# kv of two heads in column halves of the array, and the first four q units by exponentials with sums

## The chip, the core and the metric

The kernel runs on one core of a Trainium2 chip. The engines named here are TensorE (PE in the rows; PEld are its weight loads), VectorE (DVE), ScalarE (ACT), GpSimd (POOL) and SyncE (SP, which issues the transfers). The metric is the time of one execution on the device, in microseconds (us).

## What is computed

Linear attention over 8 batches, 8 heads, 576 tokens and 64 features, followed by two MLPs (512 to 2048 to 512) over the 4608 tokens. Cut to what matters here:

```
q_s = exp(q - max(q, -1));  q_s = q_s / (sum(q_s, -1) + 1e-09)
k_s = exp(k - max(k, tokens));  k_s = k_s / (sum(k_s, tokens) + 1e-09)
kv  = einsum('bhsd,bhse->bhde', k_s, v)        # 64 x 64 for each batch and head
x   = einsum('bhsd,bhde->bhse', q_s, kv)       # then (4608, 512)
x   = leaky(x @ w_in1) @ w_out1                # leaky: max(0.01 h, h)
x   = silu(x @ w_in2) @ w_out2
```

## The kernel before

**Units.** The attention works on pairs of heads. A unit is one pair p (4 of them) in one block j of 512 tokens (9 blocks); for k and v, block j stands for batch j, so that 32 units, numbered n, have a `k_task` and a `v_task`, and 36 have a `q_task`. A `k_task` loads k of both heads of one batch as four chunks of 128 tokens plus one chunk of 64 (576 = 4 x 128 + 64), finds the maximum over tokens with two transposes on TensorE (lines 480 and 486), adds its negative (489, 494), takes the exponential (498 into `kx`, 502 for the short chunk) and multiplies with v on TensorE (508 for the four chunks, 509 for the short one) into one PSUM tile `pk`. Both heads are computed in one matmul of 128 x 129: the 64 x 64 blocks on the diagonal are the two kv, the other two blocks are not read, and column 128 is a column of ones in v, whose product is the sum of the exponentials. Lines 515 and 516 form its reciprocal, and 521 scales the two blocks into `kv`.

**q.** A `q_task` finds the maximum over the 64 features (572). For the first eight units (`n < NS`) it then adds the negative maximum (577, on GpSimd or VectorE), takes one exponential of all 512 columns (581) and sums them on VectorE (583). For later units eight exponentials of 64 columns each (592) add the negative maximum as their bias and leave the sum as well. Then come the reciprocal (598, 599), the product with it (601, GpSimd or VectorE), four transposes (608), their copy (612), the matmul with kv (623), and the split of the result into two fp32r parts `x` (631 and the helper line 292).

**MLPs.** The first layer (`layer0`) is three fp32r matmuls for each of four k-tiles (651, 652, 653), for 16 columns f of w and 9 blocks. Its weights are decoded and split on ScalarE and VectorE as they come in (329 to 346, then 296 and 292). The other three layers, from about 532 us to the end, are lines 872 and 922.

**Order.** Everything is recorded by a planner, `Queues`, that holds each engine's queue as a time line and gives the next place to the task that can start first, with costs written at each `op`. Each engine then executes its rows strictly in that order. A matmul of a side task (`"p"`) may be placed between those of layer 0.

**Buffers.** Six sets of (k, v) tiles, called `u` in the rows, are lent to the units in turn. Before the first unit GpSimd writes the ones columns of v (980) and zeros the eight `kv` tiles (982).

Of the kernel before, what the change touches and what calls it, by code (L numbers as in the profile page):

```python
# [13 lines left out]
ACTF = mybir.ActivationFunctionType  # L14
# [188 lines left out]
def linear_attention_two_mlps(  # L203
# [24 lines left out]
    nc = tc.nc  # L228
    B, H, S, D = q.shape
    NT, DM = out.shape  # L230
    DFF = w_in1.shape[1]
    P = 128
    TB = 512
    NB = NT // TB
    NP = H // 2
# [3 lines left out]
    SR = S - SM  # L239
    EPS = 1e-9  # L240
    FS = 6
    NU = 8
    NS = 8
# [18 lines left out]
    gd = [tc.dram_tile([NG, 4, P, TB], F32, name=f"gd{j}") for j in range(NB)]  # L262

    NKV = 8
    NV = 2 * D + 1
    ident = const.tile([P, P], F32, name="ident")
    ones = const.tile([P, 1], F32, name="ones")
    kvbuf = [const.tile([P, P], F32, name=f"kv{i}") for i in range(NKV)]
# [166 lines left out]
    sets = []  # L435
# [9 lines left out]
    def k_task(n):  # L445

        b, j, p = units[n]
        if n >= NU:
            yield wait(("kvs", n - NU))
        of[n] = yield get(r_kv)  # L450
        kf, vv = of[n]
        done(("set", n))
        heads = slice(2 * p, 2 * p + 2)

        yield op(("D", 0.73))
        nc.sync.dma_start(
            out=kf[:, 0:512].rearrange("p (h c) -> p h c", h=2),
            in_=k[b, heads, 0:SM, :].rearrange("h (p c) d -> p h (c d)", c=4),
        )
        kh = kf[:, 0:512].rearrange("p (h c d) -> p h c d", c=4, h=2)  # L460
        k4 = kf[:, 0:512].rearrange("p (h c d) -> p c h d", c=4, h=2)
        yield op(("D", 0.56))
        k1 = kf[0:SR, 512:640]
        nc.sync.dma_start(
            out=k1.rearrange("p (h d) -> p h d", h=2), in_=k[b, heads, SM:S, :].rearrange("h p d -> p h d")
        )
        m1 = yield get(r_m)
        m2 = yield get(r_o)
        m2v = m2[:, 0:4 * D].rearrange("p (h c d) -> p h c d", h=2, c=2)
        yield op(("V", v_tt(256)))  # L470
        nc.vector.tensor_tensor(out=m2v, in0=kh[:, :, 0:2], in1=kh[:, :, 2:4], op=ALU.max)
        yield op(("V", v_tt(128)))
        nc.vector.tensor_tensor(out=m1, in0=m2v[:, :, 0], in1=m2v[:, :, 1], op=ALU.max)
        r_o.put(m2)
        m1f = m1.rearrange("p h d -> p (h d)")
        yield op(("V", v_tt(128)))
        nc.vector.tensor_tensor(out=m1f[0:SR], in0=m1f[0:SR], in1=k1, op=ALU.max)
        pm = yield get(r_attn)
        yield op(("p", 0.12))
        nc.tensor.transpose(pm[:, 0:P], m1f, ident)  # L480
        r_m.put(m1)
        nm = small[n % NU]["k"][:, 0:1]
        yield op(("V", v_tt(128)))
        nc.vector.tensor_reduce(out=nm, in_=pm[:, 0:P], axis=AX.X, op=ALU.max, negate=True)
        yield op(("p", 0.12))
        nc.tensor.transpose(pm[:, P:2 * P], nm.to_broadcast([P, P]), ident)
        nb = pm[:, P:2 * P]
        yield op(("V", v_tt(512)))
        nc.vector.tensor_tensor(
            out=k4, in0=k4,  # L490
            in1=nb.rearrange("p (h d) -> p h d", h=2).unsqueeze(1).to_broadcast([P, 4, 2, D]), op=ALU.add,
        )
        yield op(("V", v_tt(128)))
        nc.vector.tensor_tensor(out=k1, in0=k1, in1=nb[0:SR], op=ALU.add)
        r_attn.put(pm)
        kx = yield get(r_kx)
        yield op(("A", a_(512)))
        nc.scalar.activation(
            out=kx.rearrange("p (c h d) -> p c h d", c=4, h=2), in_=k4, func=ACTF.Exp
        )  # L500
        yield op(("A", a_(128)))
        nc.scalar.activation(out=k1, in_=k1, func=ACTF.Exp)
        yield wait(("v", n), *([("xm", n - NKV + NP)] if n >= NKV - NP else []))
        vv = vv.rearrange("p (c n) -> p c n", c=5)
        pk = yield get(r_attn)
        yield op(("p", 1.1))
        for c in range(4):
            nc.tensor.matmul(pk[:, 0:NV], lhsT=kx[:, c * P:(c + 1) * P], rhs=vv[:, c, :], start=c == 0, stop=False)  # L508
        nc.tensor.matmul(pk[:, 0:NV], lhsT=k1, rhs=vv[0:SR, 4, :], start=False, stop=True)  # L509
        r_kv.put(of.pop(n))  # L510
        r_kx.put(kx)
        done(("kv", n))
        rk = small[n % NU]["k"][:, 1:2]
        yield op(("V", 0.15))
        nc.vector.tensor_scalar_add(rk, pk[:, 2 * D:NV], EPS)
        nc.vector.reciprocal(out=rk, in_=rk)
        w = kvbuf[(b * NP + p) % NKV]
        for i in range(2):
            o = slice(i * D, (i + 1) * D)
            yield op(("A", a_(64)))  # L520
            nc.scalar.activation(out=w[o, o], in_=pk[o, o], func=ACTF.Copy, scale=rk[o])
        kv[b, p] = w
        r_attn.put(pk)
        done(("kvs", n))

    def v_task(n):
        b, j, p = units[n]
        yield wait(("set", n))
        t = of[n][1]
        t = t.rearrange("p (c n) -> p c n", c=5)  # L530
        for i in range(2):
            yield op(("D", 0.73))
            nc.sync.dma_start(
                out=t[:, 0:4, i * D:(i + 1) * D],
                in_=v[b, 2 * p + i, 0:SM, :].rearrange("(p c) d -> p c d", c=4),
            )

            yield wait()
        yield op(("D", 0.56))
        nc.sync.dma_start(  # L540
            out=t[0:SR, 4, 0:2 * D].rearrange("p (h d) -> p h d", h=2),
            in_=v[b, 2 * p:2 * p + 2, SM:S, :].rearrange("h p d -> p h d"),
        )
        yield wait()
        done(("v", n))
# [9 lines left out]
    def q_task(n):  # L555

        b, j, p = units[n]
# [14 lines left out]
        nc.vector.tensor_reduce(out=nq, in_=qv, axis=AX.X, op=ALU.max, negate=True)  # L572
        sq = rq = small[n % NU]["rq"]
        x4 = qx.rearrange("p (c h d) -> p c h d", c=4, h=2)
        if n < NS:
            e = yield op(("G", 1.0), ("V", v_tt(512)))
            engines[e].tensor_tensor(
                out=qv, in0=qv, in1=nq.unsqueeze(2).to_broadcast([P, 8, D]), op=ALU.add
            )
            yield op(("A", a_(512)))  # L580
            nc.scalar.activation(out=x4, in_=q4, func=ACTF.Exp)
            yield op(("V", v_tt(512)))
            nc.vector.tensor_reduce(
                out=sq, in_=qx.rearrange("p (a d) -> p a d", a=8), axis=AX.X, op=ALU.add
            )
        else:

            for c in range(4):
                for h in range(2):
                    at, to = 4 * h + c, 2 * c + h  # L590
                    yield op(("A", 0.4))
                    nc.scalar.activation(
                        out=x4[:, c, h], in_=q4[:, c, h], func=ACTF.Exp, bias=nq[:, at:at + 1],
                        accum_out=sq[:, to:to + 1],
                    )
# [379 lines left out]
    with tc.manual_schedule():  # L975
        nc.vector.memset(ones, 1.0)
        make_identity(nc, ident)
        nc.scalar.activation(out=small[0]["k"][:, 0:1], in_=ones, func=ACTF.Exp)
        for _, t in sets:
            nc.gpsimd.memset(t.rearrange("p (c n) -> p c n", c=5)[:, :, 2 * D:], 1.0)  # L980
        for t in kvbuf:
            nc.gpsimd.memset(t, 0.0)

# [58 lines left out]
```

## Time and profile before

| | |
|---|---|
| median of 3 runs | 1631.16 us (1629.92 to 1631.63) |
| the profiled execution's own time | 1635.08 us |
| its span, first to last instruction | 1633.1 us |
| mean granted TensorE clock | 0.995 |
| TensorE busy | 1603.1 us |
| VectorE, ScalarE, GpSimd busy | 1194.2, 851.3, 39.1 us |

A row of a timeline has a start, a busy time, an engine, a line of the kernel, what it writes and reads, and a count if equal rows follow each other. A row of TensorE begins when the one before it still drains, so the distance between two starts, not the busy time, is what a matmul takes of the engine. An fp32 matmul stands as two rows in the trace, an fp32r matmul as one.

### The profile page before, as it was taken

How to read it: one execution, taken by the hardware profiler on the slowest of the kernel's cores; microseconds unless marked ns; L12 is line 12 of the kernel's file. 1: busy time of each engine (PE TensorE's matmuls, PEld its weight loads, DVE VectorE, ACT ScalarE, POOL GpSimd, SP SyncE). 2: the span in 40 equal slices, each digit the busy share in tenths (PEclk: the TensorE clock that was granted, in tenths of full speed). 3: DMA queues.
4: the chain of work that ended last, by engine and by line, in shares of the span. 5: the costliest groups of instructions: out<-in, count | busy, mean ns of one | idle time of the engine just before them, and what ended most of it. 6: DMA issues, size and time to landing. Idle time of an engine off the chain costs nothing.

```text
span 1633.1 us, 30896 instructions
## 1 busy us (share of the span) xinstructions
PE 1603.1 (98%) x11456; PEld 1501.8 (92%) x11456; DVE 1194.2 (73%) x2205; ACT 851.3 (52%) x1824; POOL 39.1 (2%) x53
## 2 busy tenths in 40 slices
PE   6899999999999999999999999999999999999999
PEld 4688888888788999999999999999999999999999
DVE  8886656657566887777788966666669877777775
ACT  5768756766445544444447433444446544444442
POOL 2101001000000000000000000000000000000000
PEclk9899999999999999999999999999999999999999
DMA  8766767777779655454558344333338544444442
GB/s 227 234 195 167 209 196 240 212 242 230 225 235 311 214 150 168 141 170 145 166 143 277 131 152 140 131 133 133 135 130 279 163 131 135 133 130 136 134 132 78
DMA packets 251030, 287.25 MB, mean 176 GB/s; under 512 B 59392, under 2 KB 182272, under 8 KB 250880
## 3 DMA queue, kind: packets, MB, share of 16 engines
q1 hardware_dynamic: 250880, 285.29, 56.6%
q8 instruction: 90, 1.47, 0.4%
q14 instruction: 60, 0.49, 0.1%
HBM read 168.82 MB, written 116.39 MB: 175 GB/s over the span
## 4 chain that ended last, share of the span: by engine, by line
PE 93%; DVE 5%; DMA 1%; issue 0%; ACT 0%; SPq 0%; DVEq 0%; ACTq 0%
PE b L922 22%; PE h L922 21%; PE b L872 11%; PE h L872 11%; PE h L651 8%; PE h L653 8%; PE h L652 8%; PE a L623 2%; PE a L508 2%; PE a L608 1%; DVE o L810 1%; PE a L509 1%; DVE a L292 1%; DVE x L292 1%; DVE g L292 0%
## 5 line engine op out<-in xcount | busy, mean ns | idle before, releaser
L651 PE MATMUL h<-x,w 128*128 128x512 f32 x576 | 238.5, 414 | 2.3 <-ACT w L296 1.6
L296 ACT ACTIVATE x<-x 128x512 fp32r<-128x512 f32 x209 | 131.8, 631 | 205.8 <-DMA x<-gda 91.0
L653 PE MATMUL h<-x,w 128*128 128x512 f32 x576 | 225.9, 392 | 1.2 <-DVE w L292 1.2
L652 PE MATMUL h<-x,w 128*128 128x512 f32 x576 | 225.4, 391 | 0.8 <-DVE x L292 0.5
L810 DVE TENSOR_TENSOR o<-o,b 128x512 f32<-128x512 f32 x190 | 128.1, 685 | 72.5 <-PE b L872 39.7
L810 DVE TENSOR_TENSOR o<-o,h 128x512 f32<-128x512 f32 x188 | 126.6, 685 | 62.7 <-PE h L872 36.7
L884 ACT ACTIVATE o<-o 128x512 f32<-128x512 f32 x144 | 89.2, 629 | 145.5 <-DVE o L810 144.7
L684 ACT ACTIVATE o<-h 128x512 f32<-128x512 f32 x144 | 85.9, 597 | 118.0 <-PE h L653 109.0
L296 ACT ACTIVATE x<-o 128x512 fp32r<-128x512 f32 x169 | 105.2, 631 | 70.0 <-DVE o L810 53.8
L922 PE MATMUL b<-a,x 128*128 128x256 f32 x1080 | 141.4, 283 | 0.1
L292 DVE TENSOR_TENSOR x<-x 128x512 fp32r<-128x512 f32 x209 | 137.2, 684 | 2.5
L651 PEld LDWEIGHTS h<-x,w 128*128 128x128 f32 x576 | 108.8, 189 | 29.2 <-ACT w L296 2.5
L922 PEld LDWEIGHTS b<-a,x 128*128 128x128 f32 x1080 | 134.7, 192 | 0.3 <-DVE x L292 0.3
L922 PE MATMUL b<-x,a 128*128 128x256 f32 x1044 | 132.0, 284 | 0.6 <-DVE x L292 0.5
L653 PEld LDWEIGHTS h<-x,w 128*128 128x128 f32 x576 | 108.4, 188 | 25.6 <-DVE w L292 2.3
L872 PE MATMUL h<-x,a 128*128 128x256 f32 x1008 | 130.0, 283 | 1.3 <-DVE x L292 1.3
L652 PEld LDWEIGHTS h<-x,w 128*128 128x128 f32 x576 | 108.9, 189 | 22.8 <-issue 1.2
L922 PEld LDWEIGHTS b<-x,a 128*128 128x128 f32 x1044 | 128.1, 192 | 1.1 <-DVE x L292 1.0
L872 PEld LDWEIGHTS h<-x,a 128*128 128x128 f32 x1008 | 124.9, 192 | 1.5 <-DVE x L292 1.5
L922 PE MATMUL h<-x,a 128*128 128x256 f32 x996 | 126.0, 283 | 0.2
L872 PE MATMUL b<-x,a 128*128 128x256 f32 x960 | 123.8, 283 | 1.3 <-DVE x L292 1.3
L922 PEld LDWEIGHTS h<-x,a 128*128 128x128 f32 x996 | 122.3, 192 | 0.7 <-DVE x L292 0.6
(116 smaller groups left out, 2819.3 us busy)
## 6 DMA issues: line engine op xcount, KB each, us to landing
gda<-o SPq DMA_DIRECT2D x144, 256.0 KB, 2.6
gd<-o SPq DMA_DIRECT2D x144, 256.0 KB, 2.6
x<-gd SPq DMA_DIRECT2D x102, 256.0 KB, 2.7
x<-gda SPq DMA_DIRECT2D x89, 256.0 KB, 2.8
a<-wc SPq DMA_DIRECT2D x84, 256.0 KB, 4.3
wc<-o SPq DMA_DIRECT2D x72, 256.0 KB, 3.2
raw<-in_moe_w_out_dram SPq DMA_DIRECT2D x32, 512.0 KB, 4.2
g<-gda SPq DMA_DIRECT2D x37, 256.0 KB, 2.7
```

What stands on the lines that cost most here:

```text
L292: engines[e].tensor_tensor(out=out_, in0=a, in1=b.bitcast(F32), op=ALU.subtract)
L296: nc.scalar.activation(out=out_, in_=in_, func=ACTF.Copy)
L508: nc.tensor.matmul(pk[:, 0:NV], lhsT=kx[:, c * P:(c + 1) * P], rhs=vv[:, c, :], start=c == 0, stop=False)
L623: nc.tensor.matmul(po, lhsT=kv[bb, p], rhs=qT.rearrange("p (c t) -> p c t", c=4)[:, :, a:e], start=True, stop=True)
L651: nc.tensor.matmul(h, lhsT=w[:, 0, kk], rhs=x[:, 0], start=kk == 0, stop=False)
L652: nc.tensor.matmul(h, lhsT=w[:, 0, kk], rhs=x[:, 1], start=False, stop=False)
L653: nc.tensor.matmul(h, lhsT=w[:, 1, kk], rhs=x[:, 0], start=False, stop=kk == KD - 1)
L684: nc.scalar.activation(out=o, in_=h, func=ACTF.Prelu, alpha=0.01)
L810: nc.vector.tensor_tensor(out=o, in0=a, in1=b, op=alu)
L872: nc.tensor.matmul(bank[:, r * HB:(r + 1) * HB], lhsT=w4[:, a, r, k], rhs=x3[:, b, k], start=n == 0, stop=n == 5,)
L884: nc.scalar.activation(out=t, in_=t, func=ACTF.Silu)
L922: nc.tensor.matmul(bank[:, m * HB:(m + 1) * HB], lhsT=s[:, a, at:at + P], rhs=x[:, b, r * HB:(r + 1) * HB], start=i + m + n == 0, stop=i = ...
```

## The change

1. In `k_task` each chunk is multiplied for each head alone: 128 tokens x 64 columns of k against 65 columns of v (64 and a one), written to partitions 0 to 63 of `pk` for the first head and 64 to 127 for the second. The built program gives these matmuls a tile of 128 rows and 64 columns of the array, at column 0 and at column 64 in turn. The v tile has the ones column behind each head, so its row is 130 wide and not 129.
2. The short chunk is computed with all 128 rows: the lower 64 rows of its k and v are filled with zeros, once, by GpSimd.
3. In `q_task` units 0 to 3 now take the way with eight exponentials; units 4 to 7 keep the old one.

```
-    NV = 2 * D + 1
+    NV = 2 * (D + 1)
...
-        for c in range(4):
-            nc.tensor.matmul(pk[:, 0:NV], lhsT=kx[:, c * P:(c + 1) * P], rhs=vv[:, c, :], start=c == 0, stop=False)
-        nc.tensor.matmul(pk[:, 0:NV], lhsT=k1, rhs=vv[0:SR, 4, :], start=False, stop=True)
+        for c in range(5):
+            kc = kx[:, c * P:(c + 1) * P] if c < 4 else kf[:, 512:640]
+            for h in range(2):
+                o = slice(h * D, (h + 1) * D)
+                nc.tensor.matmul(
+                    pk[o, 0:D + 1], lhsT=kc[:, o], rhs=vv[:, c, h * (D + 1):(h + 1) * (D + 1)],
+                    start=c == 0, stop=c == 4,
+                )
...
-        nc.vector.tensor_scalar_add(rk, pk[:, 2 * D:NV], EPS)
+        nc.vector.tensor_scalar_add(rk, pk[:, D:D + 1], EPS)
...
-            nc.scalar.activation(out=w[o, o], in_=pk[o, o], func=ACTF.Copy, scale=rk[o])
+            nc.scalar.activation(out=w[o, o], in_=pk[o, 0:D], func=ACTF.Copy, scale=rk[o])
...
-                out=t[:, 0:4, i * D:(i + 1) * D],
+                out=t[:, 0:4, i * (D + 1):i * (D + 1) + D],
...
-            out=t[0:SR, 4, 0:2 * D].rearrange("p (h d) -> p h d", h=2),
+            out=t[0:SR, 4].rearrange("p (h d) -> p h d", h=2)[:, :, 0:D],
...
-        if n < NS:
+        if NP <= n < NS:
...
-        for _, t in sets:
-            nc.gpsimd.memset(t.rearrange("p (c n) -> p c n", c=5)[:, :, 2 * D:], 1.0)
+        for t_, t in sets:
+            t5 = t.rearrange("p (c h d) -> p c h d", c=5, h=2)
+            nc.gpsimd.memset(t5[:, :, :, D:], 1.0)
+
+            nc.gpsimd.memset(t_[SR:P, 512:640], 0.0)
+            nc.gpsimd.memset(t5[SR:P, 4, :, 0:D], 0.0)
```

Because the planner places every row, the order of the first part changes on all engines. On TensorE it is the same again, but for the changed matmuls, from about row 490 of 2714 on, well before layers 1 to 3. Behind line 504 the line numbers of the changed kernel are up to 10 higher (608 becomes 614, 623 becomes 629).

On TensorE, at the beginning of the program, these rows stood in a row before (480 and 486 are the transposes of k, 508 and 509 the kv of unit 0, 608 the transposes of q):

```order
L608 MATMUL a<-ident,o_154 128x128 x4
L480 MATMUL a<-ident,m_233 128x128
L486 MATMUL a<-ident,k_130 128x128
L508 MATMUL a<-u_171,kx 128x129 x4
L509 MATMUL a<-u_171,u_170 128x129
L480 MATMUL a<-ident,m_251 128x128
L608 MATMUL a<-ident,o_157 128x128 x4
L623 MATMUL a<-uq_182,kv_111 128x512
```

and these stand there now (512 is the kv, 614 the transposes of q, 629 the product of q and kv):

```order
L480 MATMUL a<-ident,m_245 128x128
L486 MATMUL a<-ident,k_130 128x128
L614 MATMUL a<-ident,o_154 128x128 x4
L480 MATMUL a<-ident,m_265 128x128
L512 MATMUL a<-u_171,kx 64x65 x8
L512 MATMUL a<-u_171,u_170 64x65 x2
L486 MATMUL a<-ident,k_133 128x128
L629 MATMUL a<-uq_182,kv_111 128x512
```

Five matmuls of a unit's kv have become ten of half the width, and the transposes of the first q stand behind those of the second k.

On ScalarE, right at the beginning, stood before (329 and 344 belong to the decoding of w, 581 is the exponential of q, 498 and 502 those of k, 612 the copy of the transposed q):

```order
L329 ACTIVATE o_155<-rw_207 128x512
L581 ACTIVATE o_154<-uq_182 128x512
L498 ACTIVATE kx<-u_170 128x512
L502 ACTIVATE u_170<-u_170 64x128
L344 ACTIVATE rw_207<-rw_207 128x512
L612 ACTIVATE uq_182<-a 128x512
```

and stands now (598 is the exponential of 64 columns with its sum):

```order
L598 ACTIVATE o_154,rq_129<-uq_182,q_128 128x64 x4
L498 ACTIVATE kx<-u_170 128x512
L502 ACTIVATE u_170<-u_170 64x128
L598 ACTIVATE o_154,rq_129<-uq_182,q_128 128x64 x4
L329 ACTIVATE o_155<-rw_219 128x512
L598 ACTIVATE o_157,rq_132<-uq_182,q_131 128x64 x5
L618 ACTIVATE uq_182<-a 128x512
```

The eight exponentials of a unit stand around those of k, and the decoding of w comes behind them.

On VectorE, at the same place, stood before (572 is the maximum of q, 484 that of k, 489 and 494 add it to k, 583 is the sum of q, 598 and 599 its reciprocal, 471 and 473 begin the next k):

```order
L572 TENSOR_REDUCE q_128<-uq_182 128x8
L484 TENSOR_REDUCE k_127<-a 128x1
L331 TENSOR_SCALAR o_155<-o_155 128x512
L489 TENSOR_TENSOR u_170<-u_170,a 128x4x2x64
L494 TENSOR_TENSOR u_170<-u_170,a 64x128
L583 TENSOR_REDUCE rq_129<-o_154 128x8
L598 TENSOR_SCALAR rq_129<-rq_129 128x8
L599 RECIPROCAL rq_129<-rq_129 128x8
```

and stands now:

```order
L578 TENSOR_REDUCE q_128<-uq_182 128x8
L484 TENSOR_REDUCE k_127<-a 128x1
L489 TENSOR_TENSOR u_170<-u_170,a 128x4x2x64
L494 TENSOR_TENSOR u_170<-u_170,a 64x128
L471 TENSOR_TENSOR o_156<-u_172 128x256
L473 TENSOR_TENSOR m_245<-o_156 128x128
L477 TENSOR_TENSOR m_245<-m_245,u_172 64x128
L578 TENSOR_REDUCE q_131<-uq_182 128x8
L604 TENSOR_SCALAR rq_129<-rq_129 128x8
L605 RECIPROCAL rq_129<-rq_129 128x8
```

The sum of q (583) is gone for this unit, the decoding of w (331) has moved back, and the second unit's k and q have moved forward.

## Rows read from the trace of the kernel before

**Rows 1.** The page: busy time of the engines, and the chain's shares.

```profile
PE 1603.1 (98%) x11456; PEld 1501.8 (92%) x11456; DVE 1194.2 (73%) x2205; ACT 851.3 (52%) x1824; POOL 39.1 (2%) x53
PE 93%; DVE 5%; DMA 1%; issue 0%; ACT 0%; SPq 0%; DVEq 0%; ACTq 0%
```

**Rows 2.** Windows: length, busy PE, PEld, DVE, ACT, POOL (rows), clock, DMA, GB/s.

```profile
0.00:72.00 72.00, 51.29 (x207) 35.92 (x208) 60.05 (x146) 44.19 (x92) 19.84 (x36) 0.91 0.82 237
72.00:112.00 40.00, 40.00 (x180) 32.77 (x179) 34.39 (x76) 25.94 (x68) 1.08 (x1) 1.00 0.71 202
```

**Rows 3.** Groups of instructions behind 72 us: count, busy us, mean ns, idle before.

```profile
L508 PE MATMUL a<-u,kx 128*128 128x129 f32 x192 | 25.4, 275 | 0.0
L509 PE MATMUL a<-u,u 64*128 64x129 f32 x48 | 11.7, 323 | 0.0
```

**Rows 4.** Timeline of PE around the kv of one unit: start, busy us.

```profile
305.35 1.05 PE L508 MATMUL a<-u,kx 128*128 128x129 f32 x8
306.34 0.49 PE L509 MATMUL a<-u,u 64*128 64x129 f32 x2
306.75 0.50 PE L651 MATMUL h<-x,w 128*128 128x512 f32 x1
307.09 0.39 PE L652 MATMUL h<-x,w 128*128 128x512 f32 x1
307.32 0.40 PE L653 MATMUL h<-x,w 128*128 128x512 f32 x1
```

**Rows 5.** Timeline of the weight loads at the same place.

```profile
306.33 0.29 PEld L509 LDWEIGHTS a<-u,u 64*128 64x128 f32 x2
306.75 0.19 PEld L651 LDWEIGHTS h<-x,w 128*128 128x128 f32 x1
306.86 0.19 PEld L652 LDWEIGHTS h<-x,w 128*128 128x128 f32 x1
```

**Rows 6.** Timeline of PE: a short product of q and kv; a transpose and its successor.

```profile
396.28 0.33 PE L623 MATMUL a<-uq,kv 128*128 128x64 f32 x2
...
124.71 0.27 PE L480 MATMUL a<-ident,m 128*128 128x128 f32 x1
124.73 0.48 PE L651 MATMUL h<-x,w 128*128 128x512 f32 x1
```

**Rows 7.** The chain that ended last, its first 80 us: start, us.

```profile
8.60 0.61 DVE rq L583
...
21.87 1.72 PE a L508 x8
23.59 0.64 PE a L509 x2
...
32.73 0.60 DVE rq L583
...
52.30 1.83 PE a L508 x8
54.13 0.73 PE a L509 x2
...
57.71 1.28 PE a L508 x8
```

**Rows 8.** Timeline of ScalarE: two exponentials with sums in a row.

```profile
104.32 0.34 ACT L592 ACTIVATE o<-uq,q 128x64 f32<-128x64 f32 x1
104.65 0.34 ACT L592 ACTIVATE o<-uq,q 128x64 f32<-128x64 f32 x1
```

**Rows 9.** Groups of instructions before 72 us: sum of q, exponential of q.

```profile
L583 DVE TENSOR_REDUCE rq<-o 128x8 f32<-128x512 f32 x8 | 5.4, 671 | 0.2 <-ACT o L581 0.2
L581 ACT ACTIVATE o<-uq 128x512 f32<-128x512 f32 x8 | 5.0, 622 | 1.3 <-POOL uq L577 1.2
```

**Rows 10.** Timeline of GpSimd: its fills of kv, and its first product with q.

```profile
1.44 1.19 POOL L982 MEMSET kv<- 128x128 f32 x8
...
9.79 1.04 POOL L601 TENSOR_TENSOR o<-o,rq 128x512 f32<-128x512 f32 x1 [2.84 <-DVE rq L599]
```

## The prediction

> **What bounds the kernel now.** I read the page first: TensorE is busy for 98% of the span, and the chain that ended last lies on it for 93% [rows 1]. A busy TensorE is not one at its peak, so the second view is the windows. From 72 us on TensorE has no gap: 40.00 of 40.00 us with VectorE at 34.39 and ScalarE at 25.94 [rows 2]. Before 72 us it is another kernel: TensorE 51.29 of 72, VectorE 60.05, ScalarE 44.19. Third, the timeline: behind 72 us the starts on TensorE follow each other without a hole, layer 0 in steps of 0.23 us (307.09 to 307.32 in [rows 4]). So there are two accounts. Behind 72 us whatever TensorE is spared is gained one for one, as long as nothing else becomes late; before, the gain goes by the chain, which runs mostly over VectorE.
>
> How many kv products lie behind 72 us: 192 rows of the four long chunks, eight to a unit, so 24 of the 32 units [rows 3].
>
> **What the kv of a unit costs now.** In [rows 4] its first row starts at 305.35 and the first layer-0 matmul that is in step again at 307.09: 1.74 us, of which 0.23 belong to the matmul at 306.75. The kv takes 1.51 us. The eight rows of the long chunks stand for 1.05 us, the last one's own 0.275 [rows 3] included, so seven steps take 0.78 and one 0.11. Ten at this pace would be 1.11; the other 0.40 is what the 64-row chunk adds: 0.99 us from 305.35 to 306.34 where eight steps are 0.89, 0.41 for two steps of 0.11, and a late step behind it (306.75 to 307.09, 0.34 for 0.23). The array is set from 128 to 64 rows and back, and the first weights behind each change can't load under the matmul before it. That weights do load under matmuls inside the other shape is in [rows 5]: two loads of 0.19 us stand for 0.29, so the second began 0.10 behind the first, and its matmul followed as in the wide shape.
>
> **What it costs afterwards.** The 64-row shape is gone (zeros filled in), but the shape of 128 rows by 64 columns takes its place, so the two changes per unit stay; I carry over their 0.40. Of it about 0.05 goes, half of one exposed load of 0.11 us (the two loads behind the change back are 0.11 apart, 306.75 and 306.86 [rows 5]), since the first load after the change has 64 columns. Remaining 0.35. The ten rows become twenty of 65 columns. The time of a row goes with its columns: 129 take 0.11, so 65 take 0.056; the shortest fp32 product here, two rows of 64 columns, stands for 0.33 us less its last row's drain of about 0.27, again 0.06 [rows 6].
>
> No row shows two halves of the array at work, so this price is bounded. From above, if the halves take turns: 20 x 0.056 = 1.12, with 0.35 it is 1.47, 0.04 less than now. From below, if a row of the second half runs wholly under one of the first: the order in a chunk is first half, first half, second, second, so that each pair of neighbours of different halves overlaps and ten full steps are left, plus ten small ones. The smallest distance of two starts is 0.02 us (124.71 to 124.73, [rows 6]): 10 x 0.076 + 0.35 = 1.11, 0.40 less. I take the halves as working at once, because they write other partitions and hold other weights and nothing else in the rows ties them, with a small step of 0.03 rather than 0.02, since the row behind 124.73 is itself late: 10 x 0.086 + 0.35 = 1.21, which is 0.30 less per unit, times 24 = **-7.2 us**.
>
> Beside these rows, TensorE: Matmul & The Clock Gate (the Trainium skill, "Part 3: Packing small matmuls") says that matmuls in other column groups start about 4 ns behind each other; by that the ten small steps would be 0.04 us together and the unit 0.95, a gain of 13 us. TensorEngine Tiling (the Trainium skill, "Key Properties") says that changing the tiling mode, though not the tile, drains the engine; here the trace agrees, with the 0.40 above, and by it my two changes per unit stay and no further one comes between the halves.
>
> **q of the first four units.** Four sums on VectorE (583) go, 0.67 us each by the mean of [rows 9]; all four stand on the chain, at 8.60 the first and at 32.73 the last, with 0.60 each [rows 7]: **-2.4 us**. The adds on GpSimd and four exponentials of 0.62 us [rows 9] go too. In return ScalarE gets 32 exponentials in steps of 0.33 (104.32 to 104.65 in [rows 8]): 2.64 us per unit for 0.62, together +8.1 us on an engine busy for 44.19 of 72 us [rows 2], while VectorE with 60.05 falls to 57. I cost that at nothing, because ScalarE has 28 us free there. The cover is thin in places: by the new order the eight exponentials of a unit stand ahead of the decoding of w (L329) and around the exponentials of k (L498), and TensorE waits for both in the end. If all of it fell on the chain it would cost 8.1; if the shorter queue on VectorE let its own waits shrink too, the gain could be 5.
>
> **kv in the first 72 us.** On the chain stand two kv products and the long part of a third: 1.72 + 0.64, 1.83 + 0.73 and 1.28, together 6.2 us [rows 7]. Shorter by a fifth (1.21 for 1.51) that is **-1.2 us**; if the halves take turns, -0.2.
>
> **Costs hidden.** GpSimd fills 18 tile parts for 6. A fill of 128 x 128 takes 1.19 / 8 = 0.15 us; the twelve more, smaller ones are at most 1.8 us, done long before its first product at 9.79 [rows 10], and its add ahead of that is gone. On SP the transfers of v now wait for these fills, with k, q and w queued behind; the fills come in the order of the units, each ahead of its transfer. Without that cover a late fill would cost what it takes, under 2 us once. The transfers have the same pieces of 64 columns. The reads of `pk` on VectorE and ScalarE keep their sizes.
>
> Sum: 7.2 + 2.4 + 1.2 = 10.8. Against the profiled execution's 1635.08 (its span 1633.1 and 2 us around it) that is 1624.3. The median of the runs shown is 3.9 lower, 1631.16, so the forecast is **1620.4 us**.
>
> **The rivals.**
> *The halves take turns* (the change doesn't do what it says). For it: one queue of loads and matmuls, and no row with two at once. Against it: only that each half is complete in itself. 24 x 0.04 + 2.4 + 0.2 = 3.6 less, 1627.6.
> *Loads are not hidden in half columns*, the one that ends on the other side. Place: inside the twenty rows. If each load of 64 columns (0.054, half of 0.11) stands bare ahead of its matmul: 20 x 0.11 + 0.35 = 2.55, 1.04 more, times 24 = +25; in the beginning 6.2 x 0.69 = +4.3, q -2.4: 1658. It decides once more than 1.51 - 0.35 - 1.12 = 0.04 us per unit is bare, less than one load. [Rows 5] speak against it, since in the 64-row shape the second load ran under the first matmul. TensorE: Matmul & The Clock Gate (the Trainium skill, "Part 3: Packing small matmuls") says that a load overlaps a running matmul only when the row group differs, and both halves here have the same rows; the second load of the 64-row pair, too, had the same rows and yet overlapped.
> *ScalarE becomes the bound at the start.* For it: 8.1 us more, in queues that VectorE waits for; against: its 28 us free. All of it on the chain gives +5.7 in place of -2.4: 1628.5 with halves at once, 1635.7 with halves in turn.
> *The half-column shape costs no change.* Then 0.35 per unit goes too, 24 x 0.65 = 15.6, and 0.65 / 1.51 of the 6.2 us at the start, 2.7; with 2.4 the sum is 20.7: 1610.5. Nothing in the rows speaks for it, the 0.40 against it.
>
> **How the numbers follow.** Halves at once 0.43; no cost of the change 0.06; halves in turn 0.27; loads bare 0.12; ScalarE 0.12. The range leaves out most of the bare loads and the far end of the fourth rival: from 1611 (small step 0.02 and a start better by 5, or no cost of the change) to 1636 (ScalarE with halves in turn). A difference under 0.2%, 3.3 us, can't be told from none here. Faster: 0.43 + 0.06 + half of the 0.27, whose 3.6 us lie at that bound, 0.62; same: the other half and half of ScalarE's, 0.20; slower: 0.18. The likeliest case's own range is 1613 to 1625.
>
> **What would show it.** Around a unit behind 72 us the distance from the first kv row to the next matmul in step should be 1.44 (1.21 and 0.23), not 1.74; the twenty rows should show starts in pairs, a short step and one of about 0.056; entry and exit should still show 0.35. Starts 0.056 apart throughout are the second case, 0.11 the third. TensorE should become full at 68 to 69 us. The sums of q on VectorE should be missing on the chain for units 0 to 3, and no exponentials of q on ScalarE should stand in their place. I would be wrong if the small step is as long as a row, or if TensorE is full only after 72 us.

## The result, and the profile after

The changed kernel takes 1611.64 us (median of 5 runs, 1611.35 to 1613.42), the kernel before 1631.16 on the same chip (5 runs, 1629.75 to 1636.43): 19.5 us less, a ratio of 0.988 with a 95% interval of 0.9864 to 0.9896. The forecast was 1620.4 in 1611 to 1636: right in its sign, 8.8 us short in its size, at the lower end of its range. The profiled execution took 1611.55, of which the span is 1609.8.

The page, its lines on the busy time of the engines and on the chain, answers to [rows 1]:

```profile
PE 1579.7 (98%) x11776; PEld 1477.8 (92%) x11776; DVE 1188.0 (74%) x2200; ACT 858.5 (53%) x1884; POOL 38.7 (2%) x62
PE 94%; DVE 3%; DMA 1%; issue 0%; SPq 0%; ACT 0%; POOL 0%; POOLq 0%; ACTq 0%; DVEq 0%
```

TensorE has 320 rows more and is busy for 23.4 us less. The windows answer to [rows 2] (length, busy PE, PEld, DVE, ACT and POOL, granted clock, DMA share, GB/s):

```profile
0.00:72.00 72.00, 50.42 (x319) 33.30 (x320) 60.91 (x154) 57.11 (x162) 18.12 (x44) 0.98 0.89 247
72.00:112.00 40.00, 40.00 (x232) 32.35 (x232) 35.99 (x86) 27.54 (x85) 2.09 (x2) 1.00 0.75 212
```

TensorE's clock in the first 72 us was granted at 0.98 where it was 0.91, and ScalarE is busy for 57.11 us in place of 44.19. VectorE, which was to fall to 57, is as busy as before in this window, with 154 rows for 146. The groups behind 72 us answer to [rows 3] (count, busy us, mean ns of one, idle before):

```profile
L512 PE MATMUL a<-u,kx 128*64 128x65 f32 x384 | 16.4, 228 | 0.0
...
L512 PE MATMUL a<-u,u 128*64 128x65 f32 x96 | 6.9, 222 | 0.0
```

A single row stands for 0.22 us, but twice as many rows as before are busy for 23.3 us together in place of 37.1: neighbours lie on top of each other. The timeline of TensorE around one unit's kv answers to [rows 4] (start, busy us, line, shape, count of rows put together):

```profile
285.96 0.39 PE L659 MATMUL h<-x,w 128*128 128x512 f32 x1
286.28 0.69 PE L512 MATMUL a<-u,kx 128*64 128x65 f32 x16
286.80 0.29 PE L512 MATMUL a<-u,u 128*64 128x65 f32 x4
287.01 0.50 PE L657 MATMUL h<-x,w 128*128 128x512 f32 x1
287.35 0.39 PE L658 MATMUL h<-x,w 128*128 128x512 f32 x1
```

From the layer-0 row at 285.96 to the one in step again at 287.35 it is 1.39 us. Two layer-0 steps of 0.23 belong to it, so the kv costs 0.93 us; 1.21 was forecast, and it was 1.51. Not merged, the twenty starts stand in pairs, 0.007 us within a pair and about 0.05 from its second row to the next pair; only the second pair comes later, 0.10 behind the first. The weight loads at the same place (against [rows 5]) run under the matmuls, sixteen and four of them in less time than the matmuls take:

```profile
286.28 0.55 PEld L512 LDWEIGHTS a<-u,kx 128*64 128x64 f32 x16 [0.35 <-issue]
286.74 0.20 PEld L512 LDWEIGHTS a<-u,u 128*64 128x64 f32 x4
```

The chain that ended last, in its first 70 us, against [rows 7] (start, us, what):

```profile
9.58 5.24 DMA uq<-in_q_dram
...
18.33 4.43 DMA u<-in_v_dram
...
25.63 1.43 ACT o L598 x8
...
48.09 0.60 DVE rq L589
...
55.39 0.61 DVE rq L589
...
65.47 0.50 PE h L659
```

The sums of units 0 to 3 are gone from it; the two that are left belong to units 4 to 7. In their place stand transfers, and once a unit's eight exponentials. From 65.47 on the chain is TensorE's.

### The profile page after: what moved, and what is told of

It is laid out like the page before. It is cut to its first block, busy times and chain, and to the rows that moved or that the text cites. A ratio compares the mean times of both kernels' runs of the same rounds, so it can differ in the third digit from the quotient of the medians.

```text
span 1609.8 us, 31563 instructions
## 1 busy us (share of the span) xinstructions
PE 1579.7 (98%) x11776; PEld 1477.8 (92%) x11776; DVE 1188.0 (74%) x2200; ACT 858.5 (53%) x1884; POOL 38.7 (2%) x62
## 3 DMA queue, kind: packets, MB, share of 16 engines
q8 instruction: 92, 1.51, 0.4%
## 4 chain that ended last, share of the span: by engine, by line
PE 94%; DVE 3%; DMA 1%; issue 0%; SPq 0%; ACT 0%; POOL 0%; POOLq 0%; ACTq 0%; DVEq 0%
PE b L928 22%; PE h L928 22%; PE b L878 11%; PE h L878 11%; PE h L657 8%; PE h L659 8%; PE h L658 8%; PE a L629 2%; PE a L512 1%; PE a L614 1%; DVE x L292 1%; DVE a L292 1%; DMA u<-in_v_dram 0%; DVE o L816 0%; DMA uq<-in_q_dram 0%
```

## The experiments

Twelve kernels ran, in three sets of four. Each set had the kernel before beside it on its chip, with medians of 1633.31, 1632.72 and 1632.17 us, so differences of 1 or 2 us between kernels of different sets are not told by medians alone. For those I use two marks in the traces: the start of unit 8's kv, the first behind 72 us, and of unit 31's, the last, 23 units later. TensorE's instructions stand in one order in the kernel before, the kv edit alone and the zeros alone, and in another, common one in the changed kernel, the q edit alone, the halves in turn, and the four kernels that do something twice; marks are compared only within such a family. Between the marks the clock is granted in full in all these kernels. Ahead of unit 8 it is not: in the traced execution of the kernel before (1635.08 us, 3.9 above its median) TensorE's clock was at 1.2 of 2.4 GHz for about 13 of the first 72 us. So a start of unit 8 held against its 111.71 measures an edit and the clock together.

| kernel | median us | ratio to before, 95% | unit 8 | unit 31 | between |
|---|---|---|---|---|---|
| before | 1631.16 | | 111.71 | 359.88 | 248.17 |
| kv edit alone | 1617.14 | 0.9893 to 0.992 | 109.17 | 344.41 | 235.24 |
| zeros alone | 1621.95 | 0.9925 to 0.995 | 108.58 | 348.19 | 239.61 |
| q edit alone | 1627.59 | 0.9957 to 0.9978 | 103.32 | 352.91 | 249.59 |
| changed | 1611.64 | 0.9864 to 0.9896 | 102.49 | 338.51 | 236.02 |
| halves in turn | 1622.78 | 0.9928 to 0.9953 | 103.08 | 348.06 | 244.98 |
| kv twice | 1627.78 | 0.9951 to 0.9978 | 104.44 | 353.87 | 249.43 |
| sums again | 1612.90 | 0.9856 to 0.9891 | 103.95 | 340.04 | 236.09 |
| subtractions again | 1613.03 | 0.9865 to 0.9896 | 102.35 | 338.37 | 236.02 |
| both again | 1613.99 | 0.9875 to 0.9909 | 103.95 | 340.04 | 236.09 |

**The kv edit alone**: the changed kernel with q as it was.

```diff
-        if NP <= n < NS:
+        if n < NS:
```

> The kv in column halves with the zeros, q as before; the order of rows on TensorE, VectorE and ScalarE is that of the kernel before. Theory (the gain is TensorE's, 0.67 us for each of the 24 units behind 72 us, plus a little in the beginning): 16 to 18 us faster, ratio 0.989 to 0.990, rows of a unit in pairs 0.007 and 0.051 apart. Rival (the new order at the start carries much of the gain): at most 13 us faster, ratio over 0.992.

Measured: 16.2 us less than before, as the theory had it. Between the marks it is 12.93 us, 0.56 for each of the 23 units, 13.5 for 24; unit 8 starts 2.54 us sooner. The forecast had 7.2 and 1.2.

**The q edit alone**: the kernel before with the other edit.

```diff
-        if n < NS:
+        if NP <= n < NS:
```

> q of units 0 to 3 by exponentials with sums, kv as before. Theory (four sums of 0.6 us go from the chain, the rest is covered): 2 to 3 us faster, ratio 0.998 to 0.999. Rival one (ScalarE becomes the bound of the start): 3 to 6 us slower, ratio over 1.002. Rival two (the shorter queue on VectorE lets its waits shrink too): 5 us or more faster, ratio under 0.997.

Measured: 5.7 us less than before where 2.4 were forecast; by its time that is rival two. But the clock takes part in it. The eight executions with the q edit alone were each granted 1.000 of it in the mean, the twelve of the kernel before beside them 0.996 to 1.000, and the three of these with 0.999 and 1.000 took 1630.23 to 1631.47 us: against them the q edit is 2.6 to 3.9 us faster. The traces show where the clock fell (the number ahead of the last two), in the kernel before:

```profile
48.00:60.00 12.00, 10.03 (x43) 7.30 (x43) 8.41 (x29) 8.31 (x20) 4.23 (x4) 0.72 0.88 281
68.00:80.00 12.00, 11.89 (x44) 9.46 (x45) 9.82 (x21) 9.26 (x19) 0.00 (x0) 0.84 0.80 213
```

and with the q edit alone:

```profile
48.00:60.00 12.00, 9.16 (x56) 6.95 (x55) 11.51 (x36) 11.02 (x26) 4.50 (x5) 1.00 0.94 288
68.00:80.00 12.00, 12.00 (x55) 9.89 (x54) 11.33 (x23) 8.03 (x15) 0.00 (x0) 1.00 0.90 231
```

Why it did not fall there is not shown. From here to the changed kernel the marks close up by 13.57 us, 0.59 per unit: kv is worth nearly the same with and without the q edit.

**The zeros alone**: the kernel before with its short chunk filled up to 128 rows, still five steps of 129 columns.

```diff
-        nc.tensor.matmul(pk[:, 0:NV], lhsT=k1, rhs=vv[0:SR, 4, :], start=False, stop=True)
+        nc.tensor.matmul(pk[:, 0:NV], lhsT=kf[:, 512:640], rhs=vv[:, 4, :], start=False, stop=True)
```

> The kernel before with one edit: the short chunk of k and v is filled with zeros to 128 rows, kv stays 128 x 129 for both heads, so no matmul of the kernel changes the shape of the array. Theory (the 0.40 us beyond ten steps of 0.11 is the change of shape and back): a unit takes 1.11, 24 x 0.40 = 9.6 us faster and about 1 in the beginning, ratio 0.993 to 0.994. Rival (the 0.40 is what a short chunk and the reading of a fresh sum cost, whatever its shape): 0 to 2 us faster, ratio over 0.998.

The median falls by 11.4 us, near the 10.6 expected. Between the marks 8.56 us go, 0.37 per unit. The timeline of one unit, with transposes on both sides:

```profile
287.82 1.06 PE L508 MATMUL a<-u,kx 128*128 128x129 f32 x8
288.72 0.39 PE L509 MATMUL a<-u,u 128*128 128x129 f32 x2
288.94 0.60 PE L608 MATMUL a<-ident,o 128*128 128x128 f32 x4
```

From 287.82 to 288.94 it is 1.12 us: ten steps of 0.11 and nothing else. The 64-row chunk, with the change of array shape that goes with it, did cost about what the prediction read out of [rows 4], 0.40.

**The halves in turn**: the changed kernel with its two loops exchanged, all ten rows of one half ahead of all ten of the other.

```diff
-        for c in range(5):
-            for h in range(2):
+        for h in range(2):
+            for c in range(5):
```

> The changed kernel with the two loops of the kv exchanged: the five chunks of the first head, then the five of the second, so that neighbours are in the same half. Theory (the gain comes from two halves at work at once, which needs neighbours in different halves): rows 0.055 apart, twenty of them 1.1, with 0.26 for the change 1.36 for a unit: 0.52 slower than the changed kernel, 24 x 0.52 = 12.5 us and about 1 in the beginning, ratio to the kernel before 0.996 to 0.997. Rival (the pairs are the two passes of one fp32 matmul, so the order of the halves is without effect): as the changed kernel, ratio 0.988.

Between the marks it is 8.96 us more than the changed kernel, 0.39 per unit, where the theory expected 0.52 and the rival nothing. So most of what two halves bring hangs on neighbours of different halves. Its timeline:

```profile
103.08 0.74 PE L512 MATMUL a<-u,kx 128*64 128x65 f32 x10
103.60 0.22 PE L512 MATMUL a<-u,u 128*64 128x65 f32 x1
103.66 0.22 PE L512 MATMUL a<-u,kx 128*64 128x65 f32 x1
103.66 0.22 PE L512 MATMUL a<-u,u 128*64 128x65 f32 x1
103.72 0.45 PE L512 MATMUL a<-u,kx 128*64 128x65 f32 x5
104.01 0.28 PE L512 MATMUL a<-u,u 128*64 128x65 f32 x2
104.22 0.32 PE L486 MATMUL a<-ident,k 128*128 128x128 f32 x1
```

From 103.08 to 104.22 it is 1.14 us; the same stretch of the changed kernel is 0.73 (286.28 to 287.01). The starts at 103.60, 103.66 and 103.72 are 0.06 apart, as the time of a row of 65 columns had been worked out.

**kv twice**: each unit's ten steps done twice in a row into the same accumulators, so that product and sum are both doubled.

```diff
-        for c in range(5):
+        for i in range(10):
+            c = i % 5
...
-                    start=c == 0, stop=c == 4,
+                    start=i == 0, stop=i == 9,
```

> The changed kernel with the ten steps of each kv unit done twice in a row into the same accumulators (both the product and the sum of the keys are doubled, so their quotient is the same). It measures a step without the change of array shape around it. Theory A (a unit of the changed kernel costs ten pairs of halves at 0.058 us, that is 0.58, and 0.35 us for the two changes of array shape): 0.58 us more for each of the 24 units behind 72 us, 13.9 us, and up to 0.58 for each of the eight before, so 1625.5 to 1630.1 and twenty pairs within about 1.16 us. Rival B (the steps cost 0.86 as predicted and the changes of shape only 0.07): 20.6 us more behind 72 us, 1632 or more. Rival C (the steps lie beside the loads and what is paid is almost all the change, 0.8): under 4 us more.

Between the marks 13.41 us come on, 0.583 per unit, and one unit shows it:

```profile
299.32 0.69 PE L513 MATMUL a<-u,kx 128*64 128x65 f32 x16
299.84 0.29 PE L513 MATMUL a<-u,u 128*64 128x65 f32 x4
299.95 0.64 PE L513 MATMUL a<-u,kx 128*64 128x65 f32 x16
300.42 0.29 PE L513 MATMUL a<-u,u 128*64 128x65 f32 x4
300.64 0.50 PE L658 MATMUL h<-x,w 128*128 128x512 f32 x1
```

From 299.32 to 300.64 it is 1.32, 0.59 more than in the changed kernel for twenty rows more. A step of both halves is 0.058 us; ten are 0.58. Of a unit's 0.93 there are 0.35 left for going into the shape and out of it, as theory A had it.

**Units in pairs**: the kv of units 4 to 31 issued two at a time, so that two units share the change of shape.

```diff
+        held[n] = kx, kf, vv, pk
+        done(("held", n))
+        if n < NP or n % 2:
+            group = (n,) if n < NP else (n - 1, n)
+            yield wait(("held", group[0]))
+            yield op(("p", 1.1 * len(group)))
...
+        else:
+            yield wait(("mm", n))
```

> The changed kernel with the kv of units 4 to 31 issued two at a time: the even unit's ten steps wait for the odd unit's operands and stand directly ahead of the odd unit's, so that the two share one change of array shape on the way in and one on the way out. The order around them moves with it. Theory A (a change in and out costs 0.35 us each time): 14 changes fewer, 12 of them behind 72 us and one of those pairs stands together in the changed kernel already, so 11 times 0.35, 3.9 us faster than the changed kernel, 1607.8 us, with 0.05 to 0.1 us between the last row of one unit and the first of the next. Rival B (the even unit's kv comes later, its q product and the layer behind it wait, or VectorE's and ScalarE's order is upset): 2 to 8 us slower than the changed kernel, with new waits of TensorE between 80 and 400 us.

The median is 1612.87, 1.2 us above the changed kernel's and not to be told from it: neither theory's time. Behind 80 us TensorE has about 3.4 us less to do, near the 3.9 of theory A, and before it loses about 3.1 more (its starts against the usual step of each kind of row, summed over both traces). These 3.1 are not the new waits of rival B: in the first 80 us TensorE is as busy as in the changed kernel (58.55 and 58.42 us). What differs is the clock, from 40 to 60 us with the pairs

```profile
40.00:60.00 20.00, 16.24 (x127) 12.88 (x127) 18.60 (x47) 13.53 (x29) 7.46 (x7) 0.77 0.79 243
```

and in the changed kernel:

```profile
40.00:60.00 20.00, 16.37 (x121) 12.20 (x122) 18.48 (x54) 15.52 (x36) 7.73 (x7) 0.93 0.77 236
```

The 0.16 between them are 3.2 of the 20 us. Why the clock was lower for longer with these pairs is not shown.

**Pairs from unit 8 on**: the same, with the first eight units left alone.

```diff
-        if n < NP or n % 2:
-            group = (n,) if n < NP else (n - 1, n)
+        if n < NS or n % 2:
+            group = (n,) if n < NS else (n - 1, n)
```

> The changed kernel with the kv of units 8 to 31 issued two at a time, the first eight units as in the changed kernel. With pairs from unit 4 on, TensorE lost about 3.1 us more than the changed kernel in the first 80 us and about 3.4 us less behind them. Theory A (the loss came from the pairs of units 4 to 7, where TensorE waits for operands, and the gain from the shared change of array shape): 3 to 3.9 us faster than the changed kernel, 1607.7 to 1608.6. Rival B (the order that the pairs upset behind 80 us gives part of it back): 1609.5 to 1612.

It takes 1608.79 us (1607.96 to 1610.06), 0.2 above the range of theory A, a ratio of 0.9855 (0.9839 to 0.9871) to before: the fastest of all, 2.9 us under the changed kernel by medians and 3.6 by the spans (1606.2 for 1609.8), though the two intervals overlap. A pair in its timeline:

```profile
105.86 0.69 PE L518 MATMUL a<-u,kx 128*64 128x65 f32 x16
106.38 0.29 PE L518 MATMUL a<-u,u 128*64 128x65 f32 x4
106.50 0.64 PE L518 MATMUL a<-u,kx 128*64 128x65 f32 x16
106.96 0.29 PE L518 MATMUL a<-u,u 128*64 128x65 f32 x4
107.18 0.32 PE L486 MATMUL a<-ident,k 128*128 128x128 f32 x1
```

Two units stand from 105.86 to 107.18, 1.32 us in place of twice 0.73, and one way in and one way out of the shape are saved besides.

**Sums again**: the changed kernel, with the sum of the exponentials of units 0 to 3 computed once more on VectorE, unused. The order of all other instructions is the same.

```diff
+        if n < NP:
+            nc.vector.tensor_reduce(out=again, in_=qv, axis=AX.X, op=ALU.add)
```

> The changed kernel, with the sum of the exponentials computed once more by VectorE for each of the first four units, just before its reciprocal (into a tile that nobody reads; the order of all other instructions is as in the changed kernel). It puts the four VectorE sums that the change took away (about 0.65 us each) back where they stood and leaves everything else. Theory A (the gain of the q edit is that these sums stood on the chain that sets the end): about 4 times 0.6 us comes back, 2.4 us, so 1614.0 us against the changed kernel's 1611.6. Rival B (the sums were beside other work; the gain is the subtraction of the maximum that VectorE also lost, or the shorter way to the transposes as ScalarE has it): within 0.6 us of the changed kernel, 1611.0 to 1612.2. Rival C (VectorE's load in the first 70 us as such, with TensorE's granted clock falling once it waits for longer): 4 us or more, with the granted clock of 40 to 80 us at 0.95 or less.

Unit 8 starts 1.46 us later, and the median is 1.3 higher. So the sums were on the way to the end, but with 1.5 us, not with 2.4. Rival C, with 4 us or more, falls, and the granted clock of 40 to 60 us (0.91) is near the changed kernel's 0.93.

**Subtractions again**: the same with GpSimd's subtraction of the maximum.

```diff
+        if n < NP:
+            nc.gpsimd.tensor_tensor(
+                out=again.rearrange("p (a d) -> p a d", a=8), in0=qv,
+                in1=nq.unsqueeze(2).to_broadcast([P, 8, D]), op=ALU.add,
+            )
```

> The changed kernel, with the subtraction of the maximum done once more by GpSimd for each of the first four units, where the kernel before had it, into a tile that nobody reads; the order of TensorE, VectorE and ScalarE is as in the changed kernel. It puts the four GpSimd rows (1.12 us each) back that the q edit took away, and no work of VectorE. In the traces a VectorE row that is under way while such a GpSimd row runs lasts about 0.72 us longer than the same row elsewhere (in the kernel with the kv edit alone the 128x128 maximum at 26.96 us took 1.02 us and others of its line 0.27). Theory A (these stretched VectorE rows are the part of the q edit's gain that the sums don't explain): up to 4 times 0.72, 2.9 us, slower than the changed kernel, 1613.0 to 1614.5, with eight to eleven stretched VectorE rows in the first 66 us where the changed kernel has eight. Rival B (the rows are stretched but VectorE is not what the start waits for then): 1611.0 to 1612.2.

Unit 8 starts 0.14 us sooner than in the changed kernel. The median is 1.4 higher, at the edge of theory A's range, but the profiled span's 1.1 us more arise behind 480 us, where the two kernels don't differ. So by the trace rival B holds: these four rows cost the start nothing. But they put back little of what theory A is about. Counting the VectorE rows of the first 66 us that overlap a GpSimd row of over 0.9 us and last 0.3 us longer than the median of their line, there are 7 here, 4.3 us too long together; 6 with 3.6 in the changed kernel; and 10 with 7.1 with the kv edit alone.

**Both again**: sums and subtractions together.

> The changed kernel with both put back for the first four units, results unused: the sum of the exponentials by VectorE just before the reciprocal, and the subtraction of the maximum by GpSimd. With that, what the q edit took away from VectorE (four sums of 0.67 us and four stretches of 0.72 us, 5.5 us) is there again, and only the eight exponentials with sums differ from the kernel with the kv edit alone, which took 1617.1 us. Theory A (the q edit's gain is VectorE's time in the first 66 us): 1615.5 to 1617.5. Rival B (GpSimd's rows cost nothing): as with the sums alone, 1612.3 to 1613.5.

(The two edits above in one kernel.) Unit 8 starts at 103.95, just as with the sums alone, and 1.60 later than with the subtractions alone, which tells the price of the sums a second time. The median, 1613.99, lies between the two theories, nearer to B; two of the five executions, 1615.97 and 1616.25, lie in A's range. This kernel has the four sums and the four subtractions back and is still 3.2 us faster than the kv edit alone by medians (2.0 if each is held against the kernel before beside it), 4.5 by the spans. That speaks against theory A, but the GpSimd rows hold VectorE up by 4.6 us here, counted as above, and by 7.1 with the kv edit alone, so not all of VectorE's load is back. What is different between these two is the place where TensorE becomes full. Their windows, with the kv edit alone:

```profile
60.00:68.00 8.00, 5.48 (x34) 3.65 (x35) 7.87 (x18) 7.16 (x16) 0.93 (x1) 0.85 1.09 364
68.00:80.00 12.00, 12.00 (x51) 9.64 (x51) 9.89 (x21) 7.80 (x16) 0.00 (x0) 0.96 0.74 184
```

and with both again:

```profile
60.00:68.00 8.00, 8.00 (x44) 5.43 (x38) 7.87 (x19) 7.79 (x18) 0.00 (x0) 0.79 1.08 360
68.00:80.00 12.00, 12.00 (x54) 9.90 (x53) 11.49 (x23) 8.64 (x16) 0.00 (x0) 1.00 0.93 237
```

From 60 to 80 us the clock was granted no higher in the second (1.7 us of full clock are gone in either), so it isn't the clock that tells them apart there; from 48 to 60 us it was 0.86 with the kv edit alone and 1.00 with both again. TensorE stands still for 2.5 of the 8 us in the first, nearly all in one wait, for ScalarE's copy of layer 0's weights (the bracket gives the idle time and what ended it):

```profile
65.53 0.75 PE L657 MATMUL h<-x,w 128*128 128x512 f32 x1 [2.22 <-ACT w L296]
66.08 0.63 PE L658 MATMUL h<-x,w 128*128 128x512 f32 x1
66.51 0.63 PE L659 MATMUL h<-x,w 128*128 128x512 f32 x1
```

Right behind the wait layer 0 goes in steps of 0.43 us (66.08 to 66.51) in place of 0.23: from 65.7 to 68.9 the granted clock is 0.50.

**q of all eight units** by exponentials with sums:

```diff
-        if NP <= n < NS:
+        if n < 0:
```

> The changed kernel with q of units 4 to 7 by ScalarE's exponentials with sums too. In the trace of the changed kernel the chain between 46 and 65 us goes almost wholly by VectorE, with two sums of these units on it (48.09 and 55.39, 0.60 us each), while ScalarE is busy 54.2 of the first 68 us. Theory A (VectorE is what the start waits for after 46 us): two to four sums go, and the subtractions with them, 1.2 to 2.4 us faster than the changed kernel, 1609.2 to 1610.4. Rival B (ScalarE, with 4 times (8 times 0.338 less 0.65), 8.2 us, more work in the same stretch, becomes what is waited for): 2 to 6 us slower than the changed kernel, 1613.6 to 1617.6, with ScalarE on the chain between 45 and 70 us.

It takes 1617.2 us, 5.6 more than the changed kernel. TensorE's clock between 60 and 80 us was granted at 0.77, and how much of the 5.6 us is the clock's is not told apart. Rival B: the chain there goes over ScalarE, with rows like these.

```profile
54.11 0.87 ACT o L598 x5
...
57.17 0.99 ACT o L598 x6
58.74 1.27 POOL o L607
```

**q of the first eight units on VectorE**, without GpSimd:

```diff
-            e = yield op(("G", 1.0), ("V", v_tt(512)))
+            e = yield op(("V", v_tt(512)))
...
-        e = yield op(("G", 1.0), ("V", v_tt(512)))
+        e = yield op(*[("G", 1.0)][n < NS:], ("V", v_tt(512)))
```

> The changed kernel with GpSimd out of the first eight units: VectorE does the four subtractions of the maximum and the eight products with the reciprocal itself (0.68 us each; GpSimd took 1.12 us each). The planner's order moves with it. Theory A (a GpSimd row costs VectorE 0.72 us of standing still, as much as the work itself, and the way by GpSimd is 0.45 us longer): no slower than the changed kernel, 1609.6 to 1612.2. Rival B (only eight of the twelve GpSimd rows stretch a VectorE row, 4.1 us in all, so VectorE has 12 times 0.68 less 4.1, 4 us, more to do in the stage that it bounds): 2 to 4 us slower, 1613.6 to 1615.6.

It takes 1618.22 us, 6.6 more, beyond both theories. The planner's order moved with it, and nearly a third of its chain between 40 and 72 us lies on a transfer of layer-0 weights (`rw`). What part is VectorE's load and what part the order can't be said from this run.

## Why the prediction was right in sign and short in size

**kv behind 72 us, the step that failed.** The mechanism held: halves at once, the change of shape still paid, loads hidden. The term that was mis-sized is the small step, "0.03 rather than 0.02": a step of both halves was put at 0.086 and is 0.058, so that the second half costs next to nothing on top of the first. Ten steps are 0.58 where 0.86 stood in the sum, the unit 0.93 where 1.21 stood, and the gain of 24 units 13.5 to 14.2 us where 7.2 stood. The small step itself is 0.007. The 0.35 for the shape, the other term of the unit, was right: 0.37 when only the zeros take a shape away, 0.93 - 0.58 = 0.35 when the steps are doubled, and about 0.31 each for eleven changes saved by the pairs (3.4 us). I had bounded the small step from below by the smallest distance in [rows 6], which are rows of the whole array; they say nothing of two halves. TensorE: Matmul & The Clock Gate (the Trainium skill, "Part 3: Packing small matmuls") gave about 4 ns, from which I had estimated 0.95 for the unit and 13 us; by that the trace nearly agrees (0.007, 0.93 and 13.5 to 14.2). The rule on loads in the same section of the Trainium skill, which would have made the change slower, this case does not bear out: no load of a half column stands bare, twenty of them lie between 286.28 and 286.94.

**The range.** The 1611.64 lies below the 1613 to 1625 of the case taken as likeliest. It lies in the stated range because of the bound at 1611, and that the bound stood there is luck: a small step of 0.02 and 5 us more at the start add 2.4 and 5 to the 10.8, which makes 1613.0, so 1611 rests on the rival without a cost of shape alone, which the runs refute.

**The halves in turn** as a rival came as a kernel of its own when the two loops were exchanged. A unit then gains 0.20 against the kernel with the q edit alone (249.59 to 244.98 between the marks), more than the 0.04 worked out, since the halves still overlap where they meet: some rows of the second half run ahead of their turn (below).

**q, half understood.** Of 2.4 us forecast, the sums brought 1.5. The edit as a whole brought 5.5 by the medians of two sets (1617.14 to 1611.64), 3.4 if each is held against the kernel before beside it. Costing ScalarE's added work at nothing was right for four units, though once it does stand on the chain (25.63), which the prediction had excluded; for eight units the chain goes over it, as the rival had it. The other 2 to 4 us are not VectorE's sums, and four GpSimd rows put back as such did not bring them back. With the old way TensorE waits 2.22 us for `w` at 65.53, and with the new one it doesn't. Three things are left that can bring `w` sooner: the subtraction no longer stands between the maximum and the exponentials, GpSimd holds VectorE up less, and the planner puts VectorE's and ScalarE's instructions in another order. Part can be the clock, which the prediction did not count: 3.4 us of full clock are gone between 48 and 80 us with the kv edit alone (0.86 to 60 us, 0.85 to 68, 0.96 to 80), and 1.7 in the changed kernel (0.86 from 36 to 48 us). No run took these apart, so that stays open.

**kv in the first 72 us.** Forecast 1.2; unit 8 starts 2.54 us sooner without the q edit, and 0.83 sooner with it. Neither is a clean measure: the zeros alone, which do less, bring unit 8 forward by 3.13 in the same order of rows, and the clock fell in the traces of the kernel before, of the kv edit alone and of the changed kernel, but not in that of the q edit alone. The fills were costed at nothing; with both edits the chain's first 6 us go over them, and on to 23 us over SP's issues and the transfers. What they cost there was not tried. TensorE is full at 65.5 us, earlier than the 68 to 69 said.

**The rival without a cost of shape** (1610.5) came nearest to the time, by its number alone: its mechanism is refuted by the pairs, the zeros and the doubling, which each find a change at 0.31 to 0.37 us. A time that fits doesn't choose between mechanisms; the timeline of one unit does.

## What to carry to other kernels

Where a product has independent halves of 64 columns, put each in its own half of the array and issue them alternately: the second was nearly free here, and issued one after the other they lost 0.39 of the 0.58 us gained per unit. Count the changes of array shape (here 0.31 to 0.37 us for one in and out), fill short chunks with zeros to avoid them, and set products of the same odd shape next to each other. Read the granted clock beside the steps: between 48 and 80 us, where TensorE has gaps, 6.8 us of full clock were gone in the kernel before and none with the q edit alone. A cost that no row shows should keep both ends in the sum until a run with the operation doubled has measured it.

## What the runs showed of the hardware that was not expected

**Rows out of the order of the program.** In the kernel with the halves in turn the program has eight rows of `kx` and two of `u` for one half, then the same for the other. The timeline has ten rows of `kx` ahead of the first `u` (103.08, x10), and five more `kx` only after the second `u` of the first half has started (103.66): two rows of the second half, at least, began before the last two of the first. All 24 units behind 72 us show it. So TensorE here started matmuls of a free half ahead of older ones of the other, and what was said above, that each engine executes its rows strictly in the order of the program, does not hold for rows of two halves.

**A VectorE row is held up while GpSimd works.** With the kv edit alone GpSimd has a product from 26.79 to 27.84:

```profile
26.79 1.05 POOL L607 TENSOR_TENSOR o<-o,rq 128x512 f32<-128x512 f32 x1 [4.11 <-DVE rq L605]
```

The VectorE maximum that starts in it ends at 27.98 and takes 1.02 us, where rows of its line take 0.345 in the mean between 66 and 400 us:

```profile
26.96 1.02 DVE L473 TENSOR_TENSOR m<-o 128x128 f32<-128x128 f32 x1
```

```profile
L473 DVE TENSOR_TENSOR m<-o 128x128 f32<-128x128 f32 x24 | 8.3, 345 | 0.5
```

SBUF — State Buffer (the Trainium skill, "Who interferes with whom") says that a VectorE instruction with two inputs in SBUF contends with a GpSimd instruction that reads SBUF, over ports that only one of them holds at a time, and that the order of issue decides which one blocks; by that the trace agrees, the later row ends 0.14 us behind the earlier one. What it costs a whole kernel is not shown: four more GpSimd rows left unit 8 where it was, but they held up only one VectorE row more.
